# Reordering two stretches of an attention and GEGLU kernel: an out tile ahead of the first spread, and wide scores ahead of block 2's

## Chip, cores and metric

One core of one Trainium2 chip. The time is the device time of one execution in microseconds (us). Profiled executions also have a trace of every instruction on TensorE (PE, its weight loads PEld), VectorE (DVE), ScalarE (ACT), GpSimd (POOL) and the DMA queues. Trace times count from the first instruction. L186 means line 186 of the kernel.

## The reference

```python
# q, k, v: (8, 8, 576, 64) float32; w_gate, w_val: (512, 1536); w_out: (1536, 512)
scores = q @ k.T / 8 + alibi bias;  kept where 0 <= i - j < 128
attn   = exp(scores - max) / sum
x      = (attn @ v), heads side by side: (4608, 512)
out    = (gelu(x @ w_gate) * (x @ w_val)) @ w_out        # (4608, 512)
```

The kernel works on groups of 512 tokens of the second half and on blocks (batch entries) of the first, and puts the attention of later blocks between the out tiles of a group.

## The kernel before

These are the parts that matter here. Every result of TensorE goes to one of 8 PSUM banks, which a pool hands out.

```python
def bank():
    ps = psum.tile([128, 512], FP32, name="ps")          # pool of 8
    ...
def scores2(b, later=None): ...   # block 2's scores of all four pairs: two banks, ScalarE exp, mask
def scores(b, s, cs, then=None, later=None):              # wide scores of the pairs cs: two banks each
    ...
            for i in (0, 1):
                exp(P[:, i, :], ps[i])                    # L193, ScalarE
            ...
            if later is None:
                mask(*args)                               # L196, VectorE: P *= emask
            else:
                later.append(args)
def sums(b, s):                                           # TensorE L308: sums over the masked P
    ps = bank()
    ...
    nc.vector.reciprocal(row(b)[:, lo:hi], ps[:, 0:hi - lo])            # L314
def spread_pe(b, s, copies=(nc.scalar.copy, nc.vector.tensor_copy)):
    pss = [bank() for _ in range(4)]
    ...                                                   # L334: reciprocals to all partitions
    for c, ps in enumerate(pss):
        copies[c % 2](out=recip[b][:, c, lo:hi], in_=ps[:, 0:hi - lo])  # L340
def values(b, s, cs=range(4)): ...                        # L351, then L357 on VectorE: xT = ps * recip
def out_half(g, u):
    t, half = u // 2, u % 2
    if half == 0:
        acc[g] = bank()
    ...                                                   # six matmuls 128x512, L393
    if half == 1:
        osb = o_pool.tile([128, DM], FP32, name="osb")
        (nc.vector.tensor_copy if g < 2 and t < 2 else nc.scalar.copy)(out=osb, in_=po)   # L398
    ...
todo = {
    0: [("s2", 1), ("s", 1, 0, (0, 1)), 0, 1, ("s", 1, 0, (2, 3)), 2,
        ("s", 1, 1, (0, 1), None, masks), 3, ("sum", 1, 0), ("masks",),
        ("s", 1, 1, (2, 3)), 4, ("spread", 1, 0, (act, act)), 5, ("transposes", 2), ("sum", 1, 1),
        ("pv", 1, 0), 6, ("spread", 1, 1, (act, act)), ("pv", 1, 1), 7],
    1: [...],          # the same pattern, with block 3's scores in between
```

A number in the list is a half out tile (`out_half`); "masks" flushes the masks put off; `(act, act)` lets ScalarE make all four copies of a spread, which ScalarE and VectorE otherwise share by turns. Each of the four "pairs" is a pair of heads. "Block 2's scores" (`scores2`, "s2") are those of the third tile of 128 tokens inside one batch entry; in "block 3's scores" the number is that of the batch entry. L186 is a score matmul, L157 a copy of transposed q or k out of PSUM (qT, kT), L370 a gate or value matmul, with which a group's work begins. The schedule is the program's order on each engine.

The softmax here doesn't subtract the row's maximum and nothing guards it: scores larger than these inputs give would overflow.

## Time and profile before

| | before |
|---|---|
| time, median of 3 runs (range) | 358.93 us (358.82 to 359.0) |
| TensorE busy in the profiled span of 357.4 us | 97% |
| waits of TensorE that the change aims at | 0.50 + 0.41 + 0.41 us |

TensorE is nearly always busy, so a change of order can only win its few idle times. The lines that show them stand in the prediction below. A row of a timeline reads: start, length, engine, line, operation, tiles, shapes, count, and in brackets the idle time before the row with what ended it. A row of the waits reads: who waited for whom, total, times, longest.

### The profile page before, as it was taken

To read this page: it belongs to the slowest core of one execution; us is meant where nothing else is said; L and a number is where in the kernel's file an instruction comes from. 1 tells how busy PE (TensorE), PEld (TensorE's weight loads), DVE (VectorE), ACT (ScalarE), POOL (GpSimd) and SP (SyncE) were. 2 spreads that over 40 slices of the span, in tenths; PEclk is the share of its full clock that TensorE was granted. 3 is DMA by queue.
4 is the path that set the end of the run, shared out by engine and by line. 5 is a ranking of instruction groups with operands and counts; after the bars stand their busy time and mean duration, and the time that the engine had idled before them with its cause. 6 is when DMAs were issued, how large, how long until landed. Compare 5 with 4: busy or idle time off the path is not lost.

```text
span 357.4 us, 7028 instructions
## 1 busy us (share of the span) xinstructions
PE 347.6 (97%) x2811; PEld 174.8 (49%) x2855; DVE 188.7 (53%) x327; ACT 186.0 (52%) x342; POOL 103.5 (29%) x137
## 2 busy tenths in 40 slices
PE   8899999999999999999999999999999999999995
PEld 3668445444454445445454545445444444444443
DVE  5676478434888646656546554745474403403320
ACT  4974495536878366632973287337833133313322
POOL 8853479501930084002910192004000000000000
PEclk9999999999999999999999999999999999999999
DMA  8999999999999199683997499759205020011002
GB/s 95 181 195 196 202 153 198 139 138 184 143 148 179 34 179 177 109 182 63 144 195 168 87 135 199 141 126 93 84 13 132 25 95 1 2 60 57 2 29 88
DMA packets 145888, 42.62 MB, mean 119 GB/s; under 512 B 131608, under 2 KB 138776, under 8 KB 145856
## 3 DMA queue, kind: packets, MB, share of 16 engines
q0 software_dynamic: 106624, 18.88, 70.2%
q1 hardware_dynamic: 36432, 17.31, 21.8%
q10 hardware_dynamic: 2800, 5.99, 7.6%
q8 instruction: 22, 0.36, 0.4%
q14 instruction: 10, 0.08, 0.1%
HBM read 43.65 MB, written 9.53 MB: 149 GB/s over the span
## 4 chain that ended last, share of the span: by engine, by line
PE 89%; DVE 4%; ACT 4%; issue 2%; DVEq 0%; ACTq 0%
PE ps L370 50%; PE ps L393 23%; PE ps L351 5%; PE ps L186 4%; ACT P L193 2%; DVE r L314 2%; PE ps L70 2%; PE ps L308 2%; PE ps L147 1%; PE ps L334 1%; PE ps L407 1%; DVE kT L157 1%; PE ps L292 1%; PE ps L278 0%; DVE hT L377 0%
## 5 line engine op out<-in xcount | busy, mean ns | idle before, releaser
L377 DVE TENSOR_TENSOR hT<-ps,gelu 128x512 bf16<-128x512 f32 (+2 forms) x115 | 74.4, 654 | 108.0 <-PE ps L370 93.1
L376 ACT ACTIVATE gelu<-ps 128x512 bf16<-128x512 f32 (+2 forms) x115 | 65.2, 572 | 115.8 <-PE ps L370 114.6
L370 PE MATMUL ps<-xT,wv 128*128 128x512 bf16 (+2 forms) x453 | 111.4, 366 | 0.6
L370 PE MATMUL ps<-xT,wg 128*128 128x512 bf16 (+2 forms) x444 | 110.4, 366 | 0.8
L393 PE MATMUL ps<-wo,hT 128*128 128x512 bf16 x402 | 94.9, 380 | 0.8
L193 ACT ACTIVATE P<-ps 128x512 bf16<-128x512 f32 x144 | 73.4, 626 | 7.7 <-PE ps L186 7.6
L370 PEld LDWEIGHTS <-wv 128*128 128x128 bf16 x460 | 44.7, 98 | 48.8
L370 PEld LDWEIGHTS <-wg 128*128 128x128 bf16 x460 | 43.2, 98 | 47.1 <-issue 0.3
L196 DVE TENSOR_TENSOR P<-P,emask 128x1024 bf16<-128x1024 bf16 (+1 forms) x79 | 49.0, 641 | 30.7 <-ACT P L193 30.2
L393 PEld LDWEIGHTS <-hT 128*128 128x128 bf16 x420 | 38.8, 98 | 47.9 <-issue 4.0
L99 POOL DMA_DIRECT2D vb<-in_v_dram x40 | 33.9, 882 | 7.8 <-PE ps L370 3.6
L398 ACT COPY osb<-ps 128x512 f32<-128x512 f32 x31 | 18.6, 601 | 29.6 <-PE ps L393 28.7
L590 POOL COPY mark<-hT 1x2 bf16<-1x2 bf16 x4 | 0.7, 176 | 98.8 <-DVE hT L377 98.8
L357 DVE TENSOR_TENSOR xT<-ps,rb 128x320 bf16<-128x320 f32 (+1 forms) x64 | 24.6, 448 | 6.8 <-DMA rb<-rd 2.9
L314 DVE RECIPROCAL r<-ps 128x320 f32<-128x320 f32 (+1 forms) x14 | 26.8, 1936 | 1.4 <-PE ps L308 1.4
L99 POOL DMA_DIRECT2D qs<-in_q_dram x30 | 25.2, 852 | 7.6 <-DMA wo<-in_moe_w_out_dram 5.1
L99 POOL DMA_DIRECT2D ks<-in_k_dram x30 | 25.3, 873 | 1.0 <-DMA qs<-in_q_dram 0.7
L186 PE MATMUL ps<-qT,kT 64*128 64x256 bf16 (+1 forms) x384 | 21.9, 244 | 1.6 <-DVE kT L157 1.1
L186 PEld LDWEIGHTS <-kT 64*128 64x128 bf16 x384 | 13.2, 94 | 13.6 <-issue 10.0
L351 PE MATMUL ps<-P,vb 128*64 128x128 bf16 (+2 forms) x384 | 18.1, 243 | 0.1
L351 PEld LDWEIGHTS <-vb 128*64 128x64 bf16 x384 | 14.7, 110 | 5.2 <-issue 4.8
L70 PE MATMUL ps<-zeros 128*128 128x512 bf16 x24 | 8.8, 485 | 1.3 <-DVE zeros L418 1.2
(65 smaller groups left out, 115.9 us busy)
## 6 DMA issues: line engine op xcount, KB each, us to landing
out_dram<-osb SPq DMA_DIRECT2D x35, 256.0 KB, 3.5
rb<-rd ACTq DMA_DIRECT2D x10, 576.0 KB, 7.3
vb<-in_v_dram POOLq DMA_DIRECT2D x32, 128.0 KB, 7.0
qs<-in_q_dram POOLq DMA_DIRECT2D x24, 128.0 KB, 5.6
ks<-in_k_dram POOLq DMA_DIRECT2D x24, 128.0 KB, 6.1
wo<-in_moe_w_out_dram POOLq DMA_DIRECT2D x2, 768.0 KB, 17.5
wg<-in_moe_w_gate_dram POOLq DMA_DIRECT2D x2, 384.0 KB, 9.5
wv<-in_moe_w_val_dram POOLq DMA_DIRECT2D x2, 384.0 KB, 10.6
```

The costliest lines, as they stand in the source:

```text
L99: nc.gpsimd.dma_start(out=t[lo:128, j, :].rearrange("p (h d) -> p h d", h=H), in_=src[b][:, 128 * j - 64 + lo:128 * j + 64, :].rearrange(" ...
L186: nc.tensor.matmul(out=ps[:, col:col + 128 * n].rearrange("p (n t) -> p n t", n=n), lhsT=blocks(kT, b, i, c, j, 1).rearrange("p n t -> p ( ...
L193: nc.scalar.activation(out=dst, in_=src, func=AF.Exp, scale=0.125)
L196: nc.vector.tensor_tensor(out=dst, in0=dst, in1=m, op=ALU.mult)
L314: nc.vector.reciprocal(row(b)[:, lo:hi], ps[:, 0:hi - lo])
L351: nc.tensor.matmul(out=ps[64 * i:64 * i + 64, a:e], lhsT=vb[b % 2][:, j, 64 * h:64 * h + 64], rhs=prob(b, s, c, i, j, e - a), start=(j == ...
L357: nc.vector.tensor_tensor(out=xT[:, c, b * S + lo:b * S + hi], in0=ps[:, 0:hi - lo], in1=recip[b][:, c, lo:hi], op=ALU.mult)
L370: nc.tensor.matmul(out=ps[:, 0:hi - lo], lhsT=w[:, c, 128 * f:128 * (f + 1)], rhs=xT[:, c, t0 + lo:t0 + hi], start=(c == 0), stop=(c == 3))
L376: nc.scalar.activation(out=gl[:, 0:hi - lo], in_=pg[:, 0:hi - lo], func=AF.Gelu)
L377: nc.vector.tensor_tensor(out=hid[g][:, f, lo:hi], in0=pv[:, 0:hi - lo], in1=gl[:, 0:hi - lo], op=ALU.mult)
L393: nc.tensor.matmul(out=po, lhsT=hid[g][:, f, 128 * t:128 * (t + 1)], rhs=wo[:, f, :], start=(f == 0), stop=(f == NF - 1))
L398: (nc.vector.tensor_copy if g < 2 and t < 2 else nc.scalar.copy)(out=osb, in_=po)
```

## The change

The intent is to let TensorE do an out tile while VectorE makes the first reciprocal (groups 0 and 1), and in group 0 to do wide scores while the last transposes are copied.

```diff
-        0: [("s2", 1), ("s", 1, 0, (0, 1)), 0, 1, ("s", 1, 0, (2, 3)), 2,
+        0: [("s", 1, 0, (0, 1)), ("s2", 1), 0, 1, ("s", 1, 0, (2, 3)), 2,
             ("s", 1, 1, (0, 1), None, masks), 3, ("sum", 1, 0), ("masks",),
-            ("s", 1, 1, (2, 3)), 4, ("spread", 1, 0, (act, act)), 5, ("transposes", 2), ("sum", 1, 1),
+            ("s", 1, 1, (2, 3)), 4, 5, ("spread", 1, 0, (act, act)), ("transposes", 2), ("sum", 1, 1),
...
-            ("s", 2, 1, (2, 3)), 4, ("spread", 2, 0), ("s2", 3, masks), 5,
+            ("s", 2, 1, (2, 3)), 4, 5, ("spread", 2, 0), ("s2", 3, masks),
```

## The prediction

> **What bounds the kernel now.** I began with the page's busy times and the chain that ended last: TensorE is busy 97% of the span and carries 89% of that chain. Only TensorE's own idle time can be won, so next I read what TensorE waited for, and then the two stretches that the diff touches on each engine's timeline.
>
> ```profile
> PE 347.6 (97%) x2811; PEld 174.8 (49%) x2855; DVE 188.7 (53%) x327; ACT 186.0 (52%) x342; POOL 103.5 (29%) x137
> PE ps L70 <- DVE zeros L418: 1.2, 1, 1.2
> PE ps L186 <- DVE kT L157: 1.1, 3, 0.5
> PE ps L334 <- DVE r L314: 0.8, 2, 0.4
> ```
>
> The second and third waits are the targets. TensorE's timeline places them (start, length, instruction, count, idle time before it with its releaser):
>
> ```profile
> 46.78 0.67 PE L186 MATMUL ps<-qT,kT 64*128 64x128 bf16 x10 [0.50 <-DVE kT L157]
> 57.00 0.82 PE L334 MATMUL ps<-r,sel 32*128 32x320 f32 x8 [0.41 <-DVE r L314]
> 59.15 0.70 PE L308 MATMUL ps<-P,ones 128*32 128x128 bf16 x24
> ...
> 96.53 0.82 PE L334 MATMUL ps<-r,sel 32*128 32x320 f32 x8 [0.41 <-DVE r L314]
> ...
> 99.01 0.61 PE L186 MATMUL ps<-qT,kT 64*128 64x256 bf16 x8
> ```
>
> The idle times before the score matmuls (L186) and before the two first spreads (L334) add to 0.50 + 0.41 + 0.41 = 1.32 us: the most that the change can win. Whether it wins them depends on VectorE, which makes what TensorE asks for next:
>
> ```profile
> 54.07 0.69 DVE L398 COPY osb<-ps 128x512 f32<-128x512 f32 x1 [0.58 <-PE ps L393]
> 54.70 2.16 DVE L314 RECIPROCAL r<-ps 128x320 f32<-128x320 f32 x1
> 56.77 2.43 DVE L196 TENSOR_TENSOR P<-P,emask 128x1024 bf16<-128x1024 bf16 x4
> 59.89 1.76 DVE L314 RECIPROCAL r<-ps 128x256 f32<-128x256 f32 x1 [0.69 <-PE ps L308]
> ...
> 94.22 2.16 DVE L314 RECIPROCAL r<-ps 128x320 f32<-128x320 f32 x1
> 96.30 2.43 DVE L196 TENSOR_TENSOR P<-P,emask 128x1024 bf16<-128x1024 bf16 x4
> 98.64 0.88 DVE L340 COPY rb<-ps 128x320 f32<-128x320 f32 x2
> ```
>
> VectorE runs without a gap from 54.07 to 59.20, and from 93.60 to 99.52. In group 0 the second sum (L308, 59.15) reads the four masked tiles that are finished at 59.20: its first three matmuls start at 59.153 to 59.160, the fourth only at 59.253, 0.05 us after the last mask ended. So that sum already runs at VectorE's heels and has no slack.
>
> **What the Trainium skill says.** "Perfetto Trace Analysis", section Optimization Strategy, advises finding the gaps on the contended engine and what releases them; that is the reading above, and the trace agrees that such gaps exist (1.32 us). The same page, section Tensor Engine Instruction, says that a matmul's reported end is estimated; I therefore work with starts. "PSUM — Partial Sum Buffer", section Engine vs sequencer instructions, says that VectorE and ScalarE queues are strict FIFO and that matmuls start in program order; the trace agrees, as the copies at 98.64 follow the masks that end at 98.73 although their input was there at about 97.3. "PSUM — Partial Sum Buffer", section Specifications, gives 8 banks; this kernel uses all 8 as a pool, so a moved tile changes who must release whose bank.
>
> **Part 1: scores of two pairs ahead of block 2's (group 0 only).** Before, the block-2 scores start at 45.81 and stop after three pairs for the last kT copy, whose first half ends at 46.72; they resume at 46.78, and the 8 wide score matmuls and the first out tile (47.38) follow. After, the 8 wide ones, whose inputs were copied long before, come first: 4 pairs at 0.109 us fill 45.81 to 46.25. The block-2 scores begin there; their second bank is that of the second-last kT copy (free at 46.26 + 0.06 = 46.32), the fourth pair is reached at about 46.49 and still waits for the same kT, until 46.78. But nothing is left behind it: the out tile can start 0.15 us later (as 97.463 to 97.612 in group 1, after the same narrow matmuls), at 46.93. Gain 47.38 − 46.93 = 0.45 us; the wait shrinks to 0.3, not to zero.
>
> ScalarE does not move: its table load begins at 46.47 after its own copies, and from 47.77 the exponentials run back to back, one ending each 0.49 us. The built program shows that the scores after the out tile's first matmuls at 50.62 (they start at 52.02) take, before and after, the banks of the fifth to eighth exponentials; the last of these ends at 51.79, and its bank is asked for at 52.25 − 0.45 = 51.81 and given at 51.79 + 0.05 = 51.85. That costs 0.04: the shift is now 0.41. The first sum then needs the mask ending at 53.50, asks at 53.98 − 0.41 = 53.57, and gets by with 0.02 to spare. So the VectorE chain of evacuation, reciprocal and four masks starts 0.41 earlier and ends at 59.20 − 0.41 = 58.79.
>
> **Part 2: the sixth half out tile ahead of the first spread, group 0.** Six matmuls at 0.216 = 1.30 us move ahead of the spread. In the shifted frame out tiles 4 and 5 run from 54.72 to 57.31, the spread starts at about 57.35 and its reciprocal was ready at 56.45: the 0.41 wait is gone. The spread takes 0.75, so TensorE asks for the second sum at about 58.1. That sum needs the last mask, 58.79 + 0.05 = 58.85. The wait of 0.41 comes back as one of 0.6 to 0.75 us at the sum. TensorE leaves the sum as early as VectorE lets it: 59.25 − 58.85 = 0.41 earlier, all of it from part 1. **Part 2 is worth nothing in group 0.**
>
> **Part 3: the same in group 1, and block 3's scores behind it.** Times as in the trace before. Out tiles 4 and 5 run from 94.65 to 97.25, the spread starts 0.31 after the last of these matmuls started (as 102.337 to 102.647 later), at 97.35 with its reciprocal ready at 96.38; block 3's scores at 97.35 + 0.75 = 98.10, the next wide scores at 98.10 + 0.23 = 98.34, the second of its pairs at 98.55. Unhindered that would be 0.69 ahead of the 99.24 of before (the wait, and two changes between unlike matmuls fewer). But its bank, in the built program, is the one that held the spread's second quarter, copied out by VectorE, and that copy stands behind the four masks in VectorE's queue: 98.64 to 99.13. The pair can start at 99.13 + 0.05 = 99.18; before, the same matmul started at 99.24. The gain is **0.06 us**, and a wait of up to 0.6 us appears at L186. Behind it the second sum (before 99.58) starts at about 99.51, its masks ready since 98.73. ScalarE's moved evacuation (now before the reciprocal copies) uses its idle time between 96.60 and 97.34 and what follows; its exponentials end about 0.1 later, used only at 100.8 and later, so no loss.
>
> After each of the two stretches everything is started by TensorE again (ScalarE has 0.64 us idle at 106.6), so the shifts should carry through to the end. Matmul count, DMA order and the queue of the output stores do not change.
>
> **Sum.** Group 0: 0.41. Group 1: 0.06. Together 0.47 us; 358.93 − 0.47 = 358.46, rounded to **358.5 us**.
>
> **Rivals.**
> - All three waits vanish: 1.32 us, 357.6 us. For it: each moved block is longer (1.30) than the wait (0.41). Against it: VectorE without a gap, and the fourth matmul at 59.253. I give it one chance in ten.
> - Only the 0.41 + 0.41 of the spreads counts, and the score swap nothing, since the same kT is still waited for: 358.1. Against it: 8 matmuls of 0.44 us are moved from behind that wait to before it.
> - ScalarE or a bank keeps the shift of part 1: the exponentials are a fixed train from 47.77, and two points have only −0.04 and +0.02 us of slack. If a further 0.2 were lost there, the gain would be 0.25: 358.7.
> - Something slows: in group 1 the moved evacuation delays ScalarE's exponentials, or the new bank order adds a wait. That would be some tenths, 359.1; no duration in the trace gives more.
>
> **Range and chances.** The three runs before span 0.18 us, so noise is about 0.1; the third rival sets the upper end, the second the lower: 358.1 to 358.8. Two per cent would be 7.2 us, over five times all waits concerned, so within 2% is all but sure.
>
> **What would show it.** In the changed kernel's waits: no wait of L334 for the reciprocal in either group; L186 waiting for kT about 0.3 instead of 0.50; a new wait of 0.6 to 0.75 of L308 for VectorE's masks in group 0, with the sum's fourth matmul about 0.4 earlier than 59.25; and a new wait of 0.5 to 0.6 of L186 for VectorE's copy at L340 in group 1. TensorE's first gate matmul of group 1 (65.32) should come 0.4 earlier, that of group 2 (107.77) 0.47 earlier. It is wrong if L308 in group 0 does not wait, if the scores in group 1 do not, or if the time falls below 358.1.

## The result, and the profile after

The changed kernel took 358.41 us (median of 4 runs, 358.25 to 359.08) against 358.97 us for the kernel before (4 runs, 358.82 to 359.54). The ratio is 0.9985, with a 95% interval of 0.9968 to 1.0002. Ratios are the mean time of one kernel's fast runs over that of the other's of the same rounds, so not quite the ratio of the medians quoted. Predicted were 358.5 us and 358.1 to 358.8.

By the times alone the gain is not clear of noise, and the profiled run of the changed kernel was itself a long one: 359.08 us, with a span of 357.3 against 357.4. So the trace must be read from points inside it. First the waits of TensorE, changed kernel:

```profile
PE ps L186 <- DVE kT L157: 0.6, 2, 0.4
PE ps L308 <- DVE P L196: 0.4, 1, 0.4
PE ps L186 <- DVE rb L340: 0.3, 1, 0.3
...
PE ps L147 <- DMA vb<-in_k_dram: 0.2, 1, 0.2
```

The waits of the spread (L334) are gone, and in their place stand one of the second sum (L308) for VectorE's masks and one of the scores (L186) for VectorE's copy at L340: the two that were forecast. Of the waits for kT one has gone from the list (1.1 and 3 times before). The last line is new too, but it lies in the first 14 us: this run waited longer for a load at its start. TensorE's timeline, changed kernel:

```profile
46.23 1.20 PE L186 MATMUL ps<-qT,kT 64*128 64x256 bf16 x16
47.36 2.76 PE L393 MATMUL ps<-wo,hT 128*128 128x512 bf16 x12
...
57.83 0.82 PE L334 MATMUL ps<-r,sel 32*128 32x320 f32 x8
58.58 0.30 PE L308 MATMUL ps<-P,ones 128*32 128x128 bf16 x3
59.26 0.60 PE L308 MATMUL ps<-P,ones 128*32 128x128 bf16 x21 [0.39 <-DVE P L196]
...
98.11 0.83 PE L186 MATMUL ps<-qT,kT 64*128 64x128 bf16 x13
99.19 0.38 PE L186 MATMUL ps<-qT,kT 64*128 64x256 bf16 x3 [0.26 <-DVE rb L340]
```

Group 0 starts here at 46.23, in the kernel before at 45.81: 0.42 later, before anything that the change touches. Its first out tile starts at 47.36 against 47.38, so 0.44 has been won by then. The sum's first three matmuls start at 58.58, the fourth at 59.26: TensorE came early and waited. VectorE, changed kernel:

```profile
54.08 0.69 DVE L398 COPY osb<-ps 128x512 f32<-128x512 f32 x1 [0.16 <-PE ps L393]
54.71 2.16 DVE L314 RECIPROCAL r<-ps 128x320 f32<-128x320 f32 x1
56.78 2.42 DVE L196 TENSOR_TENSOR P<-P,emask 128x1024 bf16<-128x1024 bf16 x4
...
98.65 0.88 DVE L340 COPY rb<-ps 128x320 f32<-128x320 f32 x2
```

Counted from the start of group 0, the four masks begin at 56.78 − 46.23 = 10.55, before at 56.77 − 45.81 = 10.96: 0.41 earlier, and still without a gap. In group 1 the copy at 98.65 did not move relative to that group, and the scores (99.19) follow it.

To be free of the start, I read from every trace the time A of the first score matmul of group 0 and three stretches of TensorE: D0 from A to the first gate matmul (L370) of group 1, D1 from there to the first gate matmul of group 2, D2 from there to the end. TensorE's timeline has the points, the kernel before first:

```profile
45.81 0.47 PE L186 MATMUL ps<-qT,kT 64*128 64x128 bf16 x6
65.32 1.03 PE L370 MATMUL ps<-xT,wg 128*128 128x512 bf16 x4
107.77 1.02 PE L370 MATMUL ps<-xT,wg 128*128 128x512 bf16 x4
```

```profile
65.33 1.03 PE L370 MATMUL ps<-xT,wg 128*128 128x512 bf16 x4
107.69 1.02 PE L370 MATMUL ps<-xT,wg 128*128 128x512 bf16 x4
```

Before and after: D0 19.51 and 19.10, D1 42.45 and 42.36, D2 249.62 and 249.61. **The change won 0.41 + 0.09 = 0.50 us.**

### The profile page after: what moved, and what is told of

It reads as the page before. It is cut to its first block, busy times and chain, and to the rows that moved or that the text cites. A ratio compares the mean times of both kernels' runs of the same rounds, so it can differ in the third digit from the quotient of the medians.

```text
span 357.3 us, 7072 instructions
## 1 busy us (share of the span) xinstructions
PE 350.5 (98%) x2855; PEld 175.0 (49%) x2855; DVE 188.4 (53%) x327; ACT 185.8 (52%) x342; POOL 103.3 (29%) x137
## 4 chain that ended last, share of the span: by engine, by line
PE 89%; DVE 3%; DMA 3%; POOL 3%; issue 1%; ACT 0%; POOLq 0%; ACTq 0%; DVEq 0%
PE ps L370 52%; PE ps L393 25%; PE ps L351 4%; PE ps L186 4%; DMA wv<-in_moe_w_val_dram 3%; PE ps L308 2%; DVE P L196 1%; DVE r L314 1%; PE ps L407 1%; POOL vb L99 1%; POOL vb L123 0%; POOL wg L133 0%; PE ps L334 0%; POOL ks L123 0%; DVE kT L157 0%
## 5 line engine op out<-in xcount | busy, mean ns | idle before, releaser
L370 PE MATMUL ps<-xT,wg 128*128 128x512 bf16 (+2 forms) x460 | 112.3, 366 | 0.1
L370 PE MATMUL ps<-xT,wv 128*128 128x512 bf16 (+2 forms) x460 | 112.1, 366 | 0.1
L370 PEld LDWEIGHTS <-wv 128*128 128x128 bf16 x460 | 44.6, 98 | 49.1 <-DMA wv<-in_moe_w_val_dram 0.4
L370 PEld LDWEIGHTS <-wg 128*128 128x128 bf16 x460 | 43.2, 98 | 47.1 <-issue 0.3
L186 PE MATMUL ps<-qT,kT 64*128 64x256 bf16 (+1 forms) x384 | 22.1, 244 | 1.3 <-DVE kT L157 0.6
L186 PEld LDWEIGHTS <-kT 64*128 64x128 bf16 x384 | 13.4, 94 | 13.3 <-issue 9.6
L70 PE MATMUL ps<-zeros 128*128 128x512 bf16 x27 | 9.2, 468 | 1.2 <-DVE zeros L418 1.2
```

The costliest lines, as they stand in the source:

```text
L186: nc.tensor.matmul(out=ps[:, col:col + 128 * n].rearrange("p (n t) -> p n t", n=n), lhsT=blocks(kT, b, i, c, j, 1).rearrange("p n t -> p ( ...
L370: nc.tensor.matmul(out=ps[:, 0:hi - lo], lhsT=w[:, c, 128 * f:128 * (f + 1)], rhs=xT[:, c, t0 + lo:t0 + hi], start=(c == 0), stop=(c == 3))
```

## Experiments

Eight kernels ran, in two groups of four, each group on one chip with its own runs of the kernel before. All gave the right result. "Lowest" is the shortest of a kernel's 5 or 6 runs; the runs before had 358.73 (first group) and 358.77 (second).

| kernel | median | lowest | ratio, 95% interval | A | D0 | D1 | D2 |
|---|---|---|---|---|---|---|---|
| before (first profile) | 358.93 | 358.82 | | 45.81 | 19.51 | 42.45 | 249.62 |
| swap_only | 358.75 | 358.33 | 0.9987 (0.9968 to 1.0006) | 45.40 | 19.10 | 42.45 | 249.60 |
| out5_g0_only | 359.11 | 358.75 | 1.0001 (0.9981 to 1.0021) | 46.90 | 19.51 | 42.45 | 249.60 |
| out5_g1_only | 359.12 | 358.67 | 1.0003 (0.9979 to 1.0027) | 47.80 | 19.51 | 42.36 | 249.61 |
| whole | 358.62 | 358.25 | 0.9990 (0.9968 to 1.0011) | 45.39 | 19.10 | 42.36 | 249.61 |
| evac_act | 358.71 | 358.27 | 1.0005 (0.9978 to 1.0033) | 45.74 | 19.10 | 42.36 | 249.61 |
| mask_early | 358.16 | 358.14 | 0.9976 (0.9965 to 0.9988) | 45.52 | 19.20 | 42.15 | 249.61 |
| evac_act_mask_early | 357.80 | 357.53 | 0.9965 (0.9953 to 0.9977) | 45.66 | 18.60 | 42.15 | 249.60 |
| g1_act_copies | 359.26 | 358.73 | 1.0017 (0.9999 to 1.0036) | 45.40 | 19.10 | 42.81 | 249.61 |

D2 agrees within 0.02 us in all of them, and D0 and D1 repeat to 0.01 wherever that part of the program is the same (19.10 in five traces and 42.36 in four, the changed kernel's first trace counted). A varies from 45.39 to 47.80 over instructions that are the same in all. So the noise of these traces lies before A, and the stretches can be trusted to some hundredths. The lowest times agree: 0.40 under before for the swap, 0 and 0.06 for the two out tiles, 0.48 for the whole; in the second group 0.50, 0.63, 1.24 and 0.04 from evac_act down, where the stretches give 0.50, 0.61, 1.21 and 0.05.

### swap_only: the scores alone

```diff
-        0: [("s2", 1), ("s", 1, 0, (0, 1)), 0, 1, ...
+        0: [("s", 1, 0, (0, 1)), ("s2", 1), 0, 1, ...
```

> Only the scores of two pairs go ahead of block 2's; both out tiles stay where they were. I read three stretches of TensorE: D0 from the first score matmul of group 0 to the first gate matmul of group 1 (19.51 us before), D1 from there to the first gate matmul of group 2 (42.45 before). Theory (the swap alone moves VectorE's chain): D0 = 19.10, as in the whole change, D1 = 42.45, the spread still waits 0.41 for its reciprocal, no wait at the second sum; time 0.4 under the kernel before. Rival (the order of the out tile shares in the gain of group 0): D0 between 19.10 and 19.51, clearly above 19.10.

D0 is 19.10: the whole gain of group 0. TensorE's waits from 40 to 115 us:

```profile
PE ps L334 <- DVE r L314: 0.8, 2, 0.4
```

The spreads still wait 0.4 each for the reciprocal, and in group 0 that costs nothing: D0 is as short as with the whole change. Theory held, rival refuted.

### out5_g0_only: the out tile in group 0 alone

```diff
-            ("s", 1, 1, (2, 3)), 4, ("spread", 1, 0, (act, act)), 5, ...
+            ("s", 1, 1, (2, 3)), 4, 5, ("spread", 1, 0, (act, act)), ...
```

> Only the sixth half out tile goes ahead of the first spread in group 0. Theory: worth nothing, D0 = 19.51 (within 0.03), the 0.41 wait of the spread is gone and stands as a wait of about 0.6 between the third (or an earlier) and the fourth matmul of the second sum, which starts at the same 0.05 after the last mask. Rival (the wait of the spread is really won): D0 = 19.10. Time the same as before within noise in theory, 0.4 lower in the rival.

D0 is 19.51, as before. TensorE's timeline of this kernel shows where the wait went:

```profile
58.91 0.82 PE L334 MATMUL ps<-r,sel 32*128 32x320 f32 x8
59.66 0.30 PE L308 MATMUL ps<-P,ones 128*32 128x128 bf16 x3
60.34 0.60 PE L308 MATMUL ps<-P,ones 128*32 128x128 bf16 x21 [0.38 <-DVE P L196]
```

The spread no longer waits; the sum does: its first three matmuls start at 59.66 to 59.74, the fourth at 60.34, after the mask that ended VectorE's chain at 60.29. The wait moved and nothing was won.

### out5_g1_only: the out tile in group 1 alone

```diff
-            ("s", 2, 1, (2, 3)), 4, ("spread", 2, 0), ("s2", 3, masks), 5,
+            ("s", 2, 1, (2, 3)), 4, 5, ("spread", 2, 0), ("s2", 3, masks),
```

> Only the sixth half out tile goes ahead of the first spread in group 1. Theory: D0 = 19.51, D1 = 42.45 - 0.08 = 42.37; the wait for the reciprocal is gone, a start-to-start gap of about 0.5 appears inside the next wide scores, released by VectorE's copy of the spread's second quarter. Rival (group 1 gains its whole wait): D1 = 42.0. Time 0.1 lower in theory, 0.4 in the rival; neither is told apart from noise by the time, both are by D1.

D1 is 42.36: 0.09 won, not 0.41. The gap inside the wide scores is there (timeline of TensorE):

```profile
100.09 0.83 PE L186 MATMUL ps<-qT,kT 64*128 64x128 bf16 x13
101.17 0.38 PE L186 MATMUL ps<-qT,kT 64*128 64x256 bf16 x3 [0.25 <-DVE rb L340]
```

The profiled run (361.08 us) was the longest of this kernel, all of it from the start (A 47.80).

### whole: the change again, beside its parts

```diff
+# the whole change, again
```

> The whole change again, beside its parts on the same chip. Theory: D0 = 19.10, D1 = 42.36, so 0.50 of the stretches whatever the start of the kernel does; time 0.5 under the kernel before, with single runs up to 0.8 apart because the loads at the start land at different moments. If the parts do not add (swap alone plus out tile in group 1), something else is at work.

D0 19.10 and D1 42.36. The parts add: 0.41 + 0 + 0.09 = 0.50. The single runs lay 1.34 apart (358.25 to 359.59), more than the 0.8 expected; for the cause named there see the point on noise below.

### evac_act: less work on VectorE ahead of the reciprocal

From here on each kernel is the whole change and the edit shown.

```diff
-        (nc.vector.tensor_copy if g < 2 and t < 2 else nc.scalar.copy)(out=osb, in_=po)
+        (nc.vector.tensor_copy if g < 2 and t < 1 else nc.scalar.copy)(out=osb, in_=po)
```

> The whole change, and the second out tile of groups 0 and 1 evacuated by ScalarE in place of VectorE: 0.6 us less work on VectorE just before the reciprocal. Theory: the reciprocal is then held by the end of the first sum, which ends at the same moment as that evacuation did, so VectorE's chain starts no earlier: D0 = 19.10 and D1 = 42.36, both within 0.05. Rival (VectorE's amount of work alone decides): D0 = 18.5, D1 = 41.8.

D0 and D1 stay at 19.10 and 42.36. VectorE's timeline in group 0:

```profile
54.22 2.16 DVE L314 RECIPROCAL r<-ps 128x320 f32<-128x320 f32 x1 [0.79 <-PE ps L308]
```

VectorE now idles 0.79 us, until the first sum ends; the reciprocal starts 54.22 − 45.74 = 8.48 after A, as in the changed kernel (54.71 − 46.23 = 8.48). Taking work from a chain helps only if the next link can start earlier.

### mask_early: the order on VectorE alone

```diff
-            ("s", 1, 1, (0, 1), None, masks), 3, ("sum", 1, 0), ("masks",),
+            ("s", 1, 1, (0, 1), None, masks), ("mask1",), 3, ("sum", 1, 0), ("masks",),
...   (the same in group 1)
+    def mask1():
+        mask(*masks.pop(0))
```

> The whole change, and the first of the four masks put ahead of the second out tile's evacuation on VectorE, without taking work off it. Theory: in group 0 VectorE is idle only 0.17 there after the change, and the mask's input comes late, so the chain ends 0.1 later: D0 = 19.23. In group 1 there is 0.58 of idle time: the copy that holds the scores ends about 0.28 earlier, D1 = 42.08. Rival (the wait is not for VectorE's chain): no change in either.

D0 is 19.20, 0.10 worse: in group 0 VectorE had no room for a mask. D1 is 42.15, 0.21 better than 42.36 but short of 42.08. In group 1 VectorE's copy starts 97.72 − 64.72 = 33.00 after the first gate matmul of group 1, in the changed kernel 98.65 − 65.33 = 33.32: 0.32 earlier, so the copy came as early as expected and a part of it was not used. The next kernel shows the reason.

### evac_act_mask_early: both

The diffs of the two kernels above together.

> Both together: the second out tile evacuated by ScalarE, and the first mask ahead of the reciprocal in the room that this leaves. Theory: group 0's masks end 0.5 earlier, the wait of the second sum shrinks from 0.6 to about 0.15, D0 = 18.6. In group 1 the copy ends about 0.48 earlier; part of it may be taken by ScalarE's exponentials: D1 = 41.9 to 42.05. Time about 0.8 under the whole change. Rival (VectorE is not what holds it): D0 = 19.10, D1 = 42.36.

D0 is 18.60, as forecast. VectorE's and TensorE's timelines in group 0 (A is 45.66):

```profile
53.64 0.69 DVE L196 TENSOR_TENSOR P<-P,emask 128x1024 bf16<-128x1024 bf16 x1 [0.29 <-ACT P L193]
54.25 2.15 DVE L314 RECIPROCAL r<-ps 128x320 f32<-128x320 f32 x1
56.32 1.82 DVE L196 TENSOR_TENSOR P<-P,emask 128x1024 bf16<-128x1024 bf16 x3
```

```profile
58.01 0.79 PE L308 MATMUL ps<-P,ones 128*32 128x128 bf16 x24
```

One mask fills the room, the other three end at 58.14 − 45.66 = 12.48 instead of 59.21 − 46.23 = 12.98, and the sum runs in one piece. D1 is 42.15, no better than with the mask alone and short of the expected 41.9 to 42.05, although the copy on VectorE came earlier still (97.17 − 64.26 = 32.91). The chain of waits of this kernel in group 1 tells why:

```profile
96.36 0.79 PE ps L334 x8
97.14 0.73 ACT rb L340 x2
97.88 1.98 ACT P L193 x4
...
99.90 1.46 PE ps L393 x6
```

After the spread it runs through ScalarE: two copies, then four exponentials back to back, and the out tile at 99.90 waits for the bank of the fourth. With VectorE out of the way, ScalarE's exponentials are the next limit. The changed kernel shows how near it was: there the fourth exponential ended at 100.91 and this out tile started at 101.16, so with 0.05 from end to start only 0.20 could still be won, and mask_early had won 0.21. This kernel is the fastest of all: 357.80 us, 0.9965 of the time before, and D0 + D1 is 60.75 against 61.46 for the change and 61.96 before.

### g1_act_copies: whose copy holds the scores' bank

```diff
-            ("s", 2, 1, (2, 3)), 4, 5, ("spread", 2, 0), ("s2", 3, masks),
+            ("s", 2, 1, (2, 3)), 4, 5, ("spread", 2, 0, (act, act)), ("s2", 3, masks),
```

> The whole change, with the first spread of group 1 copied out by ScalarE alone, as group 0 does. Theory: the scores' second pair no longer waits for VectorE's copy behind its masks; its last wait moves to ScalarE's copy and is about 0.2 shorter. But ScalarE's exponentials come 0.6 later, and the values behind the second sum wait for them, some 0.2 to 0.4: D1 = 42.3 to 42.5. D0 = 19.10 unchanged. Rival (the bank is not the cause): the gap inside the wide scores stays 0.5.

The gap inside the scores before it (0.52 from start to start in the changed kernel) shrinks to 0.33 and is no longer VectorE's: the bank was the cause. But D1 is 42.81, worse than expected and 0.36 worse than with no change. Its chain of waits:

```profile
97.39 1.39 ACT rb L340 x4
98.78 1.98 ACT P L193 x4
100.80 1.46 PE ps L393 x6
```

Four copies stand ahead of the same four exponentials, 0.66 us more than with two, and all of the delay comes out at the out tile: D1 is 42.81 − 42.15 = 0.66 above that of the kernel with two copies and one mask moved. I had taken the loss behind the sum for 0.2 to 0.4; it is the delay of ScalarE's whole train.

## Why the prediction was right

Each step is held against what the runs showed.

- **The bound.** TensorE's waits in two stretches, with VectorE behind them. Right for group 0: D0 moves with the end of VectorE's masks (19.10 to 18.60 as they end at 12.48 and not 12.98 after A). In group 1 ScalarE takes over once D1 is 0.21 shorter than with the change. D2, 70% of the span, does not move in any kernel.
- **Part 1, the swap: 0.45 at the first out tile, 0.41 at the end.** Right: 0.44 and 0.41, and alone it gives all of group 0. The wait for kT that was to shrink to 0.3 is too short for the list of waits: its row counts 0.13 of idle time, and from start to start the gap is 0.34 (46.86 to 47.20).
- **Part 2, worth nothing in group 0.** Right: out5_g0_only leaves D0 at 19.51, and the wait stands at the sum. Its idle time reads 0.39 in the waits and not 0.6 to 0.75, because the row counts from the modelled end of the third matmul; from start to start the gap is 0.60 (58.66 to 59.26).
- **Part 3, 0.06 in group 1.** Right in mechanism, 0.09 in size. The prediction had all of the scores' second pair wait for VectorE's copy. Only its second matmul did, at 99.19 as worked out (99.18); the first writes another bank, copied out by ScalarE until 98.61, and started at 98.67. So less was left behind the wait, and the sum started at 99.49 rather than about 99.51; in this trace, whose group 1 starts 0.01 later, that makes 0.09. The wait reads 0.26 idle, 0.52 from start to start. ScalarE's exponentials end 0.22 later (101.89 against 101.67), twice the 0.1 said; that cost nothing here, as the out tile behind them asked at 101.16 for a bank free since 100.91.
- **Shifts carry through to the end.** Right: D2 is the same within 0.02. In absolute time the gate matmuls did not come 0.4 and 0.47 earlier, as the prediction's last signs had it (65.33 after 65.32, and 107.69 after 107.77), because this trace's group 0 starts 0.42 later; counted from A they came 0.41 and 0.50 earlier.
- **Noise about 0.1.** This was too small. The three runs at hand spanned 0.18; eleven runs of the kernel before in one group spanned 358.73 to 361.04. With such noise it is partly luck that a median of four fell within 0.1 of the 358.5 said, and it is the stretches that bear the prediction out. In the traces the noise is the part before A, and no experiment here was made on its cause. They show two things: a wait of 0.2 us and one of 0.8 us for a load at about 13 us in two traces (changed kernel, out5_g0_only), and TensorE's first matmuls starting at two rates. In out5_g1_only (A 47.80) matmuls of 128x512 (L70) still start 427 ns apart between 7 and 9 us; in whole (A 45.39) the same ones start 216 ns apart from 6.3 us on, and by the scores at 12.35 against 9.94 all of the 2.41 us between the two is there. The record of the granted clock reads 1.00 in both.

That VectorE holds both waits is shown by experiment and not only read. With one mask moved into free room, and the room made by ScalarE, group 0 wins 0.50 more and the sum's wait goes; in group 1 the scores' bank changes hands when the copy does. What one would gain if ScalarE's train in group 1 were shorter stays open.

## What to carry to other kernels

Before moving work into an engine's wait, ask what the engine will ask for next and who makes it: if the same busy engine makes both things, the wait only moves behind the moved work. Follow that engine's queue in order, and look at who last held the buffer as well as at who makes the data. When a gain is smaller than the noise of whole runs, measure it in the trace between two points that the change does not touch.

## What the Trainium skill lacked or had wrong

- "TensorE: Matmul & The Clock Gate", section Back-to-back issue gap, gives about 131 ns per matmul of 512 columns for a stream of weight loads and matmuls. Here such matmuls, each with its own weight load, start 216 ns apart (six of a half out tile in 1.30 us), the figure that the page gives for isolated ones.
- "ScalarE: Activation LUTs", section What ACT_TABLE_LOAD costs, adds a drain of about 1380 ns to the 1283 ns of the load. The load agrees (1.28 us), but in the kernel before the next exponential starts at 47.77 after a load from 46.47 to 47.75, and the copy ahead of it ended at 46.45: no such drain is seen.
- None of the pages that I used gives the time from the end of one engine's instruction to the start of a matmul that waits for it. It was 0.05 us here, for VectorE's masks (59.20 to 59.25) and for its copy (99.13 to 99.19, changed kernel).
